# Sums of the second layers' weights and activations: from VectorE to GpSimd, gate halves to VectorE, activation sums begun at the last set's first output

## The chip, the core and the metric

One core of a Trainium2 chip runs the whole program. The metric is the device time of one execution in microseconds, of which three runs were timed. The engines are TensorE (PE in the rows, with its weight loads as PEld), VectorE (DVE), ScalarE (ACT), GpSimd (POOL) and SyncE (SP), which issues the transfers.

## What is computed

Attention with a memory term for 4 batches of 8 heads and 576 tokens, then two feed-forward blocks over all 2304 tokens. The change touches the end of the first block and the whole of the second:

```python
x = attn_out.transpose(0, 2, 1, 3).reshape(2304, 512)
h = x @ w_in                       # 512 -> 2048
x = maximum(0.01 * h, h) @ w_out   # 2048 -> 512
a, b = x @ w_a, x @ w_b            # 512 -> 1536 each
out = (a * b) @ w_out2             # 1536 -> 512
```

## The kernel before

Every fp32 matmul is made of three (`three`, L372 to L375): each operand is split into a rounded high half and a low half, and high x high, high x low and low x high are added in PSUM. A high half is a cast on ScalarE, a low half a subtraction (operand minus high half) on VectorE or GpSimd. So each tile that TensorE reads costs the other engines two steps, and those steps are what the order of the program is about.

The tokens go in two parts, 0 to 1023 and 1024 to 2303. The first block (`moe1`) runs over nine sets of a part with one or two of the eight groups of hidden features: `inward` gives hidden columns (leaky ReLU on ScalarE, L1077, then both halves), `outward` adds them into the result y of that part (L1095, VectorE). The last set is part 1 with groups 6 and 7: its outward part has eight outputs of 512 columns and four of 256. Beside it the program prepares the second block.

The second block (`moe2`) computes a and b for 1024 tokens of each part by a Strassen-like scheme with 7 products instead of 8. Matrices w_a and w_b come as 12 matrices of 2x2 blocks, b and a in turn; part by part the loop over q = 0 to 11 makes seven products (`product`), which take the right blocks or sums of blocks:

- `Matrices.make(m)` loads matrix m into the tile raw, forms the sums T1 to T4 of its blocks (L1257, four steps of 128x256), casts the high halves (L1260, ScalarE, tiles bhi or ahi) and subtracts the low halves (L1264, GpSimd, blo or alo), four pieces of 512 columns (p = 0 and 1 the blocks, 2 and 3 the sums), and writes the result to DRAM for the second pass over the tokens.
- `Sums` forms S1 to S4 out of the blocks of the activations (`total`, L1166) and the halves of the S and of A11, A12 and A22 (`hi` and `lo`, L1170 to L1178; L1175 for A, L1178 for S). `last` (L1145) makes the halves of a rest of 256 tokens of part 1.
- The product's results are added out of PSUM on VectorE (L1357, L1361 for product 1 on ScalarE). When an odd q is reached, `done` multiplies a and b (the gate, L1384) and `finish` casts the gate's high half (L1340) and subtracts the low half (L1342). `result` multiplies the gates with w_out2 and adds (L1419, VectorE); `Weights.final` makes the halves of w_out2 (L358 and L359).

What sets the order: every output or product is one tick. `after(k, fn)` puts a step into the program k ticks later, so each engine's queue is fixed by ticks; the engines then run through their queues in order and wait by semaphores. `jobs` is a list of steps of which `run(n)` issues n at each output or product.

PSUM has eight banks: four in turn for products and inward results (ring u), four for outputs (ring o). A bank is free again when VectorE or ScalarE has read it.

```python
for x_ in (("T1", "B12", "B11"), ("T2", "B22", "T1"), ("T3", "B22", "B12"), ("T4", "B21", "T2")):
    after(k, total(*x_))
for p in range(4):
    after(k + 1 + p, hi(p))
    after(k + 2 + p, low(p))
```

The slots of an even and an odd q in the first pass are "16572O3O4OO" and "1O6O5OO7234" (digits are products, O an output of the pair before).

Of the kernel before, what the change touches and what calls it, by code (L numbers as in the profile page):

```python
# [16 lines left out]
ALU = mybir.AluOpType  # L17
AX = mybir.AxisListType

B, H, S, D = 4, 8, 576, 64  # L20
# [92 lines left out]
def f32(ap):  # L113
    return ap.bitcast(F32)
# [3 lines left out]
def attention_moe_moe2(ctx: ExitStack, tc, kqT, qn, vn, m_prev, beta, w_in, w_out, w_a, w_b, w_o2, out):  # L118
    nc = tc.nc
# [10 lines left out]
    keep = const.tile([P, H], F32, name="keep")  # L130
# [16 lines left out]
    def after(k, fn):  # L147
        now[1] += 1
        heapq.heappush(tasks, (now[0] + k, now[1], fn))
# [969 lines left out]
    class Sums:  # L1119
# [22 lines left out]
        def last(self, y):  # L1142
            e = slice(1024, 1280)
            nc.scalar.copy(self.tail[:, 0], y[:, :, e])
            after(1, lambda: nc.gpsimd.tensor_tensor(self.tail[:, 1], y[:, :, e], f32(self.tail)[:, 0], ALU.subtract))  # L1145

        def jobs(self, y, places):

            at = self.at
            V, G = nc.vector, nc.gpsimd  # L1150

# [21 lines left out]
            def lo(x, eng):  # L1173
                if x[0] == "A":
                    fn = lambda: eng.tensor_tensor(at[x][:, 1], plain(x), f32(at[x])[:, 0], ALU.subtract)  # L1175
                else:
                    fn = lambda: [
                        eng.tensor_tensor(*two(at[x][:, 1, k], of(x, k), f32(at[x])[:, 0, k]), ALU.subtract) for k in range(2)  # L1178
                    ]
                return lambda: after(1, fn)  # L1180
# [16 lines left out]
    class Matrices:  # L1197
# [48 lines left out]
        def make(self, m):  # L1246
# [4 lines left out]
            lo = self.lo[x]  # L1251
            k = max(0, self.when + 5 - now[0])
            self.when = now[0] + k + 6

            def total(o, a, b):
                o, a, b = (self.pair(n) for n in (o, a, b))
                return lambda: nc.vector.tensor_tensor(o, a, b, ALU.subtract)  # L1257

# [11 lines left out]

            for x_ in (("T1", "B12", "B11"), ("T2", "B22", "T1"), ("T3", "B22", "B12"), ("T4", "B21", "T2")):
                after(k, total(*x_))
            for p in range(4):
                after(k + 1 + p, hi(p))
                after(k + 2 + p, low(p))
            if m < 11:
                after(k + 6, lambda: self.load(m + 1))
            after(k + 7, keep)

# [33 lines left out]
    def moe2(ps, sums, mats, spare):  # L1313
# [7 lines left out]
        for pr in range(2):  # L1321
# [16 lines left out]
            def finish(g, f, c, gf):  # L1338
                t = into(g, f)
                after(1, lambda: nc.scalar.copy(t[:, 0, c], gf))  # L1340
                eng = nc.vector if pr or (f, c.start) == (1, 0) else nc.gpsimd
                after(2, lambda: eng.tensor_tensor(t[:, 1, c], gf, f32(t)[:, 0, c], ALU.subtract))  # L1342

# [96 lines left out]
    with tc.manual_schedule():  # L1440
# [54 lines left out]
        for n, kind, g, w in moe1(ps, gates, lambda n: t31 if n == 1 else fourth(n), xs, y):  # L1495
# [3 lines left out]
            if n == len(SETS) - 1:  # L1499
                if (kind, g) == ("u", 6) and m == 1:  # L1500
# [4 lines left out]
                    mats.when = now[0]  # L1505
                if (kind, g) == ("u", 7) and m == 2:
                    m = 3
                    jobs.append(sums.jobs(ys[0], None)["1"])
                    mats.make(0)
                if kind == "o":  # L1510
                    m += 1
                if m == 9:
                    m = 10
                    while weights.items or weights.quarter or weights.spare:
# [6 lines left out]
                    sums.second()  # L1521
                    steps = sums.jobs(ys[0], {f"S{i + 1}": spares[i * 2 : i * 2 + 2] for i in range(4)})
                    jobs += [steps[k] for k in "ab65c2d7"]
                    mats.make(1)
            run(2)
            convert(w, 0.7 if n == 0 else 0.74)
# [4 lines left out]
        for pr, (kind, q, k) in moe2(ps, sums, mats, spares):  # L1531
            if (pr, kind, q, k) == (0, "P", 4, "1"):
# [6 lines left out]
                    "S4": [r[:, k * 512 : k * 512 + 512] for k in range(2, 4)],  # L1539
                })  # L1540
            if (pr, kind, q, k) == (0, "P", 6, "1"):
# [80 lines left out]
```

## Time and profile before

| | us |
|---|---|
| median of three runs | 1021.49 |
| lowest, highest | 1020.34, 1022.60 |
| the profiled execution | 1017.84 |
| its span, first to last instruction | 1016.1 |
| TensorE busy in the span | 991.3 |
| VectorE, ScalarE, GpSimd busy | 804.8, 424.2, 351.0 |

The profile is of one execution. An engine's busy time counts its instructions from start to end, a stretch in which an instruction of VectorE or GpSimd is held up by the other included. A wait is put down to the instruction that came last. The second block's products begin at about 590 us, its second pass over the tokens at about 780 us.

### The profile page before, as it was taken

What the parts mean: (1) busy time and instruction counts of PE and PEld (TensorE: products, weight loads), DVE (VectorE), ACT (ScalarE), POOL (GpSimd) and SP (SyncE); (2) the same over time, 40 slices, a digit from 0 to 9 for tenths busy, and PEclk for the clock granted to TensorE, in tenths of its full rate; (3) what the DMA queues carried; (4) which work ended last, traced back from release to release, by engine and by line L of the source; (5) the groups of instructions that cost most, each with busy time, mean ns of one, the idle gap of its engine ahead of it and who ended that gap; (6) DMA issues with size and microseconds to landing.
All of it is one profiled execution on the core that took longest, in us unless ns stands there. A gap on an engine that the chain in (4) does not pass through costs nothing. (4 is left out here: it accounts for less than half of the span.)

```text
span 1016.1 us, 14584 instructions
## 1 busy us (share of the span) xinstructions
PE 991.3 (98%) x5266; PEld 798.7 (79%) x5266; DVE 804.8 (79%) x1546; ACT 424.2 (42%) x947; POOL 351.0 (35%) x333
## 2 busy tenths in 40 slices
PE   9999999999999999999998989899998999999998
PEld 4666666788888888888887878778886888888887
DVE  6999998699798989898999585887787717647646
ACT  7988887565435242524235134323233121201201
POOL 6788777331102010202015156665555101001000
PEclk9999999999999999999999999999999999999999
DMA  7344432233435343434353344536555422432312
GB/s 228 106 133 138 154 107 73 63 125 114 145 107 174 112 137 115 160 120 145 106 162 117 118 188 175 215 123 224 221 186 188 159 111 93 149 132 94 138 50 104
DMA packets 41432, 139.88 MB, mean 138 GB/s; under 512 B 4752, under 2 KB 5520, under 8 KB 36752
## 3 DMA queue, kind: packets, MB, share of 16 engines
q1 hardware_dynamic: 41216, 138.95, 40.1%
q8 instruction: 41, 0.67, 0.3%
q14 instruction: 31, 0.25, 0.1%
q10 hardware_dynamic: 144, 0.00, 0.0%
HBM read 98.57 MB, written 40.37 MB: 137 GB/s over the span
## 5 line engine op out<-in xcount | busy, mean ns | idle before, releaser
L1357 DVE TENSOR_TENSOR gf<-b,gf 128x512 f32<-128x512 f32 x148 | 100.8, 687 | 63.5 <-PE b L375 58.8
L1419 DVE TENSOR_TENSOR xf<-b,xf 128x512 f32<-128x512 f32 (+1 forms) x91 | 61.7, 683 | 60.9 <-PE b L375 60.5
L1044 POOL TENSOR_TENSOR hl<-gf,hl 128x512 fp32r<-128x512 f32 (+1 forms) x20 | 28.3, 1415 | 233.3 <-ACT hl L1043 224.2
L373 PE MATMUL b<-xh,w 128*128 128x512 f32 x256 | 100.9, 394 | 0.0
L374 PE MATMUL b<-xh,w 128*128 128x512 f32 x256 | 99.7, 390 | 0.0
L375 PE MATMUL b<-xh,w 128*128 128x512 f32 x256 | 99.7, 389 | 0.0
L359 POOL TENSOR_TENSOR w<-bhi,w 128x512 fp32r<-128x512 f32 x24 | 35.8, 1492 | 181.2 <-ACT w L358 180.8
L373 PE MATMUL b<-xs,bhi 128*128 128x512 f32 (+1 forms) x216 | 79.7, 369 | 5.6 <-DVE gf L1357 5.1
L374 PE MATMUL b<-xs,bhi 128*128 128x512 f32 (+1 forms) x216 | 79.1, 366 | 0.0
L373 PE MATMUL b<-xs,ahi 128*128 128x512 f32 (+1 forms) x216 | 79.0, 366 | 0.0
L374 PE MATMUL b<-xs,ahi 128*128 128x512 f32 (+1 forms) x216 | 79.0, 366 | 0.0
L375 PE MATMUL b<-xs,blo 128*128 128x512 f32 (+1 forms) x216 | 79.0, 366 | 0.0
L375 PE MATMUL b<-xs,alo 128*128 128x512 f32 (+1 forms) x216 | 79.0, 366 | 0.0
L1077 ACT ACTIVATE gf<-b 128x512 f32<-128x512 f32 (+1 forms) x76 | 42.0, 553 | 82.5 <-PE b L375 80.8
L619 ACT ACTIVATE p<-p,stat 128x512 f32<-128x512 f32 (+3 forms) x128 | 71.0, 560 | 4.8 <-DVE stat L673 4.4
L373 PE MATMUL b<-hl,w 128*128 128x512 f32 (+1 forms) x176 | 65.8, 374 | 2.9 <-DVE xf L1095 2.9
L646 POOL TENSOR_SCALAR p<-p,stat,keep 128x128 f32<-128x128 f32 (+3 forms) x95 | 61.2, 656 | 16.1 <-DVE stat L634 13.7
L261 ACT ACTIVATE wh<-wraw 128x512 f32<-128x512 f32 x64 | 42.7, 668 | 55.2 <-DMA wraw<-in_w_o 21.5
L374 PE MATMUL b<-hl,w 128*128 128x512 f32 (+1 forms) x176 | 65.6, 373 | 0.0
L375 PE MATMUL b<-hl,w 128*128 128x512 f32 (+1 forms) x176 | 65.4, 372 | 0.0
L673 DVE CUSTOM_DVE_ANT_0 p<-b,mask 128x512 f32<-128x512 f32 (+3 forms) x128 | 57.6, 478 | 5.6 <-PE b L665 5.2
L302 DVE SCALAR_TENSOR_TENSOR wa<-wraw,wa 128x512 uint32<-128x512 uint32 x64 | 56.0, 875 | 1.4
(207 smaller groups left out, 2673.3 us busy)
## 6 DMA issues: line engine op xcount, KB each, us to landing
wraw<-in_w_in SPq DMA_DIRECT2D x16, 512.0 KB, 4.0
wraw<-in_w_out SPq DMA_DIRECT2D x16, 512.0 KB, 3.4
qraw<-in_qn SPq DMA_DIRECT2D x8, 768.0 KB, 7.0
wraw<-in_w_b SPq DMA_DIRECT2D x12, 512.0 KB, 3.4
wraw<-in_w_a SPq DMA_DIRECT2D x12, 512.0 KB, 3.7
plain<-wa SPq DMA_DIRECT2D x24, 256.0 KB, 3.7
wraw<-in_w_o SPq DMA_DIRECT2D x12, 512.0 KB, 3.7
raw<-plain SPq DMA_DIRECT2D x12, 512.0 KB, 3.3
```

The lines of the kernel that those rows point to most:

```text
L261: nc.scalar.activation(t["h"], self.raw[n][:, :, 1].bitcast(F32), AF.Abs)
L302: V.scalar_tensor_tensor(u["a"], raw[:, :, 1], 0xC0000000, u["a"], ALU.bitwise_and, ALU.bitwise_or)
L359: after(k + 6, lambda f=f: nc.gpsimd.tensor_tensor(w[:, 1, f], f32(stage), f32(w)[:, 0, f], ALU.subtract))
L373: nc.tensor.matmul(outp, l_hi, r_hi, start=start, stop=False)
L374: nc.tensor.matmul(outp, l_hi, r_lo, start=False, stop=False)
L375: nc.tensor.matmul(outp, l_lo, r_hi, start=False, stop=stop)
L619: nc.scalar.activation(t, t, AF.Exp, bias=s[:, 0, col : col + 1], scale=-1.0, accum_out=s[:, 1, col : col + 1])
L646: ENG[eng].tensor_scalar(live[p], live[p], stats[w % 3][:, 3, col : col + 1], k, ALU.mult, ALU.mult)
L673: nc.vector.tensor_tensor_reduce(one(p, [P, wd]), plan.tiles[banks[j]][:, c : c + wd], mask[:, off : off + wd], -0.125, BIG, ALU.add, ALU. ...
L1077: nc.scalar.activation(gf, hp[:, 0:n], AF.Prelu, alpha=0.01)
L1357: nc.vector.tensor_tensor(left[q, to], src, left[q, add], ALU.add)
L1419: nc.vector.tensor_tensor(y[:, i, c], op, y[:, i, c], ALU.add)
```

## The change

Six edits. The sums T1 to T4 go from VectorE to GpSimd and stand between the low halves of one matrix, over eight ticks. All gate low halves of the first pass go to VectorE (before, three of four were GpSimd's). For part 1 all S sums and their low halves go to GpSimd (`jobs` takes the engine as V). A's low halves and the tail's are two steps of 512 columns in place of one of 1024. Everything that prepares the second block begins at the last set's first output: the first matrix (before: at the inward part of group 7), the activation sums (before: at the sixth output), one job a tick in place of two; the second matrix follows at the seventh output. Minimum distances between matrices shrink by a tick.

```diff
@@ Sums.last
-            after(1, lambda: nc.gpsimd.tensor_tensor(self.tail[:, 1], y[:, :, e], f32(self.tail)[:, 0], ALU.subtract))
+            for k in (slice(0, 2), slice(2, 4)):
+                after(
+                    1 + 2 * k.start,
+                    lambda k=k: nc.gpsimd.tensor_tensor(self.tail[:, 1, k], y[:, k, e], f32(self.tail)[:, 0, k], ALU.subtract),
+                )
@@ Sums.jobs
-        def jobs(self, y, places):
+        def jobs(self, y, places, V):
...
-                    fn = lambda: eng.tensor_tensor(at[x][:, 1], plain(x), f32(at[x])[:, 0], ALU.subtract)
+                    fn = lambda: [
+                        eng.tensor_tensor(at[x][:, 1, k], plain(x)[:, k], f32(at[x])[:, 0, k], ALU.subtract) for k in range(2)
+                    ]
@@ Matrices.make
-            k = max(0, self.when + 5 - now[0])
-            self.when = now[0] + k + 6
+            k = max(0, self.when + 4 - now[0])
+            self.when = now[0] + k + 5
...
-                return lambda: nc.vector.tensor_tensor(o, a, b, ALU.subtract)
+                return lambda: nc.gpsimd.tensor_tensor(o, a, b, ALU.subtract)
...
-            for x_ in (("T1", "B12", "B11"), ("T2", "B22", "T1"), ("T3", "B22", "B12"), ("T4", "B21", "T2")):
-                after(k, total(*x_))
-            for p in range(4):
-                after(k + 1 + p, hi(p))
-                after(k + 2 + p, low(p))
+            steps = [
+                [hi(0), hi(1)], [low(0)], [total("T1", "B12", "B11"), total("T2", "B22", "T1")], [low(1), hi(2)],
+                [total("T3", "B22", "B12"), total("T4", "B21", "T2")], [hi(3), low(2)], [], [low(3)],
+            ]
+            for n, fns in enumerate(steps):
+                for fn in fns:
+                    after(k + n, fn)
             if m < 11:
-                after(k + 6, lambda: self.load(m + 1))
-            after(k + 7, keep)
+                after(k + 5, lambda: self.load(m + 1))
+            after(k + 8, keep)
@@ finish
-                eng = nc.vector if pr or (f, c.start) == (1, 0) else nc.gpsimd
-                after(2, lambda: eng.tensor_tensor(t[:, 1, c], gf, f32(t)[:, 0, c], ALU.subtract))
+                after(2, lambda: nc.vector.tensor_tensor(t[:, 1, c], gf, f32(t)[:, 0, c], ALU.subtract))
@@ the last set
-                if (kind, g) == ("u", 7) and m == 2:
-                    m = 3
-                    jobs.append(sums.jobs(ys[0], None)["1"])
-                    mats.make(0)
                 if kind == "o":
                     m += 1
                 if m == 9:
-                    m = 10
+                    mats.make(1)
+                if m == 3:
...
                     sums.second()
-                    steps = sums.jobs(ys[0], {f"S{i + 1}": spares[i * 2 : i * 2 + 2] for i in range(4)})
-                    jobs += [steps[k] for k in "ab65c2d7"]
-                    mats.make(1)
-            run(2)
+                    mats.make(0)
+                    steps = sums.jobs(ys[0], {f"S{i + 1}": spares[i * 2 : i * 2 + 2] for i in range(4)}, nc.vector)
+                    jobs += [steps[k] for k in "a1b65c2d7"]
+            run(2 if n == 0 else 1)
...
-                })
+                }, nc.gpsimd)
```

How the queues move, in three places (names: xf the result y, gf and raw sums and products, xs and hl halves that TensorE reads, b a PSUM bank). VectorE, the last set's outputs, before:

```order
L1095 TENSOR_TENSOR xf<-b_5869,xf 128x512
L1166 TENSOR_TENSOR gf<-xf 128x512 x2
L1166 TENSOR_TENSOR gf<-gf,xf 128x512 x2
L1257 TENSOR_TENSOR raw<-raw 128x256 x4
L1095 TENSOR_TENSOR xf<-b_5904,xf 128x512
L1178 TENSOR_TENSOR xs_5890<-gf,xs_5890 128x512 x4
L1095 TENSOR_TENSOR xf<-b_5928,xf 128x512
```

and now, from the first output on:

```order
L1095 TENSOR_TENSOR xf<-b_5780,xf 128x512
L1170 TENSOR_TENSOR gf<-xf 128x512 x2
L1095 TENSOR_TENSOR xf<-b_5809,xf 128x512
L1095 TENSOR_TENSOR xf<-b_5828,xf 128x512
L1170 TENSOR_TENSOR gf<-gf,xf 128x512 x2
L1095 TENSOR_TENSOR xf<-b_5846,xf 128x512
L1184 TENSOR_TENSOR xs_5801<-gf,xs_5801 128x512 x2
L1095 TENSOR_TENSOR xf<-b_5866,xf 128x512
```

Where twelve steps stood between the additions of three outputs, six now stand between those of five, and the sums of weights are gone from the queue.

GpSimd from the second matrix to the third, around the first products of the second block, before:

```order
L1264 TENSOR_TENSOR alo<-raw,ahi 128x512 x2
L1175 TENSOR_TENSOR xs_5890<-xf,xs_5890 128x1024
L1264 TENSOR_TENSOR alo<-raw,ahi 128x512 x2
L1175 TENSOR_TENSOR xs_5516<-xf,xs_5516 128x1024
L359 TENSOR_TENSOR w<-bhi,w 128x512
L1264 TENSOR_TENSOR blo<-raw,bhi 128x512 x4
```

and now:

```order
L1270 TENSOR_TENSOR alo<-raw,ahi 128x512
L1263 TENSOR_TENSOR raw<-raw 128x256 x2
L1270 TENSOR_TENSOR alo<-raw,ahi 128x512
L1263 TENSOR_TENSOR raw<-raw 128x256 x2
L1270 TENSOR_TENSOR alo<-raw,ahi 128x512
L1180 TENSOR_TENSOR xs_5516<-xf,xs_5516 128x512 x2
L1270 TENSOR_TENSOR alo<-raw,ahi 128x512
L359 TENSOR_TENSOR w<-bhi,w 128x512
L1270 TENSOR_TENSOR blo<-raw,bhi 128x512
L1263 TENSOR_TENSOR raw<-raw 128x256 x2
```

Two sums stand behind each matrix's first and second low half, and A22's low half (xs) before the last; the third matrix goes on in the same way, with a step of w before its last low half.

VectorE at the first gates (the end of q = 1), before:

```order
L1384 TENSOR_TENSOR gf<-raw,gf 128x512
L1357 TENSOR_TENSOR gf<-b_6135,gf 128x512
L1384 TENSOR_TENSOR gf<-gf 128x512
L1357 TENSOR_TENSOR gf<-b_6149,gf 128x512
L1384 TENSOR_TENSOR gf<-gf 128x512
L1357 TENSOR_TENSOR gf<-b_6163,gf 128x512
L1384 TENSOR_TENSOR gf<-gf 128x512
L1342 TENSOR_TENSOR hl_6132<-gf,hl_6132 128x512
```

and now:

```order
L1391 TENSOR_TENSOR gf<-raw,gf 128x512
L1364 TENSOR_TENSOR gf<-b_6138,gf 128x512
L1391 TENSOR_TENSOR gf<-gf 128x512
L1349 TENSOR_TENSOR hl_6133<-gf,hl_6133 128x512
L1364 TENSOR_TENSOR gf<-b_6151,gf 128x512
L1391 TENSOR_TENSOR gf<-gf 128x512
L1349 TENSOR_TENSOR hl_6147<-gf,hl_6147 128x512
L1364 TENSOR_TENSOR gf<-b_6164,gf 128x512
L1391 TENSOR_TENSOR gf<-gf 128x512
L1349 TENSOR_TENSOR hl_6133<-gf,hl_6133 128x512
L1349 TENSOR_TENSOR hl_6147<-gf,hl_6147 128x512
```

One low half behind four gates has become four, of which two stand before the fourth product's sum.

## Rows read from the trace of the kernel before

**Rows 1.** The page, span and part 1: busy us, share of the span, instructions.

```profile
span 1016.1 us, 14584 instructions
PE 991.3 (98%) x5266; PEld 798.7 (79%) x5266; DVE 804.8 (79%) x1546; ACT 424.2 (42%) x947; POOL 351.0 (35%) x333
```

**Rows 2.** Waits of TensorE from 540 us on: total us, times, longest.

```profile
PE b L373 <- DVE gf L1357: 5.1, 2, 3.1
PE b L374 <- DVE xs L1044: 3.7, 1, 3.7
PE b L373 <- DVE xf L1095: 2.9, 1, 2.9
PE b L373 <- DVE xf L1419: 1.4, 1, 1.4
PE b L375 <- POOL qs L1342: 1.4, 1, 1.4
PE b L373 <- ACT qs L1340: 1.1, 1, 1.1
PE b L373 <- DVE raw L1357: 0.4, 1, 0.4
PE b L375 <- DVE hl L1342: 0.2, 1, 0.2
```

**Rows 3.** Windows: length, TensorE busy us (instructions), granted clock, transfer share, GB/s.

```profile
555.00:560.00 5.00, 1.32 (x7) 0.98 0.00 0
560.00:565.00 5.00, 5.00 (x16) 0.68 0.97 326
```

**Rows 4.** Timeline, last set's inward part: start us, us, engine, line, step.

```profile
543.06 2.64 POOL L1175 TENSOR_TENSOR xs<-xf,xs 128x1024 fp32r<-128x1024 f32 x1 [1.09 <-ACT xs L1170]
543.36 2.63 DVE L1044 TENSOR_TENSOR hl<-gf,hl 128x256 fp32r<-128x256 f32 x1
547.06 3.61 DVE L1257 TENSOR_TENSOR raw<-raw 128x256 f32<-128x256 f32 x4
```

**Rows 5.** Timeline of TensorE: first matmuls of inward, outputs, q = 0, q = 1.

```profile
542.82 0.40 PE L373 MATMUL b<-xh,w 128*128 128x512 f32 x1
...
553.72 0.39 PE L373 MATMUL b<-hl,w 128*128 128x512 f32 x1
...
589.92 0.40 PE L373 MATMUL b<-xs,bhi 128*128 128x512 f32 x1
...
599.47 0.39 PE L373 MATMUL b<-xs,ahi 128*128 128x512 f32 x1
```

**Rows 6.** Timeline of VectorE, last set's outputs.

```profile
580.87 6.87 DVE L1178 TENSOR_TENSOR xs<-gf,xs 128x512 fp32r<-128x512 f32 x4
```

**Rows 7.** Timeline of VectorE, first pass of the second block.

```profile
645.58 6.27 DVE L1257 TENSOR_TENSOR raw<-raw 128x256 f32<-128x256 f32 x4
...
677.08 3.48 DVE L1166 TENSOR_TENSOR xf<-xf 128x512 f32<-128x512 f32 x2
```

**Rows 8.** Prices: timeline rows, a source line (ns min/median/max), two groups (busy us, mean ns).

```profile
757.93 0.68 DVE L1178 TENSOR_TENSOR xs<-raw,xs 128x512 fp32r<-128x512 f32 x1
675.37 1.78 DVE L1342 TENSOR_TENSOR hl<-gf,hl 128x512 fp32r<-128x512 f32 x1
592.33 1.30 POOL L1264 TENSOR_TENSOR alo<-raw,ahi 128x512 fp32r<-128x512 f32 x1 [5.14 <-ACT ahi L1260]
607.99 1.75 POOL L1342 TENSOR_TENSOR hl<-gf,hl 128x512 fp32r<-128x512 f32 x1 [1.92 <-ACT hl L1340]
L1257 DVE TENSOR_TENSOR raw<-raw x48: 409/422/2001, 547.1 to 744.6; 128x256 f32<-128x256 f32 x48
L1044 POOL TENSOR_TENSOR hl<-gf,hl 128x256 fp32r<-128x256 f32 x1 | 0.9, 854 | 3.8 <-DVE hl L1044 3.8
L1357 DVE TENSOR_TENSOR gf<-b,gf 128x512 f32<-128x512 f32 x148 | 100.8, 687 | 63.5 <-PE b L375 58.8
```

**Rows 9.** Timeline of VectorE, end of the first pass.

```profile
772.98 3.98 DVE L1166 TENSOR_TENSOR raw<-xf,raw 128x512 f32<-128x512 f32 x2
```

More of the change, by code (lines that the diff above doesn't have):

```diff
@@ L1144, in last @@
             nc.scalar.copy(self.tail[:, 0], y[:, :, e])
-            after(1, lambda: nc.gpsimd.tensor_tensor(self.tail[:, 1], y[:, :, e], f32(self.tail)[:, 0], ALU.subtract))
-        def jobs(self, y, places):
+            for k in (slice(0, 2), slice(2, 4)):
[4 more added lines that the diff above has]
+        def jobs(self, y, places, V):
             at = self.at
-            V, G = nc.vector, nc.gpsimd
+            G = nc.gpsimd
             def plain(x):
```

## Prediction

> **What bounds the kernel now.** I read the page first: TensorE is busy in 991.3 us of a span of 1016.1 [rows 1], so little but its idle stretches can be won. The waits of TensorE come second. From 540 us on they add up to 16.3 us in nine waits [rows 2]; the reader is to see that six of the eight rows name VectorE as what was waited for, one GpSimd and one ScalarE, and none a transfer. All of it lies in the part of the program that the change reorders. The windows come third: the granted clock reads 1.00 all through, except 0.98 and 0.68 in the ten microseconds after the first of these waits [rows 3]; 0.02 and 0.32 of 5 us each are 1.7 us lost at the lower of the two levels (1.2 GHz). It followed a wait of 3.7 us; the waits of 3.1 and 2.9 us were followed by none.
>
> The timelines come last, for why VectorE was late. A subtraction of two SBUF operands of 128x512 takes 0.68 us on VectorE when GpSimd is quiet and 1.78 us when it is not [rows 8]; four sums of weights (T1 to T4) took 3.61 us in one place and 6.27 us in another, although the median of one is 422 ns [rows 4, 7, 8]. VectorE's steps with one PSUM operand don't show this: 148 of them average 687 ns [rows 8]. So VectorE is late where its SBUF steps stand in bunches beside a busy GpSimd, and TensorE then lacks a half or a free bank.
>
> **The change, part by part.** TensorE's order is not touched. The sum is made against the profiled execution: 1017.84 us, with 1016.1 us of span. The three runs' median is 1021.49, 3.65 above it; I take the difference from the median.
>
> *The last set's inward part.* The high and low halves of A11 and the first matrix's sums go away from here: on VectorE 3.61 us of sums and a step held for 2.63 us behind a GpSimd step of 2.64 us [rows 4]. VectorE's low half that TensorE waited for began at about 559.1 us, its input long ready; with some 5 us less ahead of it and GpSimd nearly quiet, it is done before TensorE arrives. I take all of the wait, 3.7 us, and with it the 1.7 us of low clock: **-5.4**.
>
> *The last set's outputs.* They begin at 553.72 us [rows 5], and the activation sums now begin at the first of them instead of the sixth. Before, four low halves took 6.87 us beside GpSimd [rows 6], VectorE's additions stood behind them and TensorE ran out of banks. Four inward outputs take 553.72 - 542.82 = 10.90 us [rows 5], so one of 512 columns takes 2.72. Now each has one addition (0.69) and at most two SBUF steps, which with one GpSimd step in the way of each are 2 x 1.78: 4.2 us at worst for single outputs, 2.0 at best, and four banks to spread it over. I count no wait: **-2.9**. If the cover is gone, one bank's worth, 2.7, comes back.
>
> *The steady part, first pass.* Per pair of matrices VectorE loses eight sums (8 x 0.42) and gains three low halves (3 x 0.68), and the second pass's sums and halves leave it (16 steps). The bunches behind the waits named gf and raw of L1357 (the 6.27 us, and 3.48 us for two sums of activations [rows 7]) no longer stand on VectorE: 5.1 + 0.4 us, **-5.5**.
>
> *The end of the first pass.* Four waits, 1.4 + 1.4 + 1.1 + 0.2 = 4.1 us [rows 2]. One goes: the 3.98 us of S4's sum that held up the additions [rows 9] move to GpSimd. But after the last four products VectorE now makes all four low halves itself, in order: from the end of product 7 the steps are two sums, a gate, then three times sum, gate and half, so the half of product 2 is ready 9 x 0.68 = 6.1 us later, that of product 3 8.2 us later. TensorE wants them 4.5 and, once moving, 0.7 us after the former: waits of 1.6 and 1.4, plus up to 1.1 for one step of GpSimd's in the way. I take 3.6 for 4.1: **-0.5** (between -1.1 and +2).
>
> *What is late next: GpSimd at the start of the second layers.* With the waits gone TensorE starts these 3.7 + 1.7 + 2.9 = 8.3 us earlier, at 589.92 - 8.3 = 581.6 [rows 5], while GpSimd's work is later and longer. From the second matrix's first low half to the last of the third matrix its queue holds twelve steps of 512 columns and eight sums. A low half takes 1.30 us alone [rows 8]. No sum has run on GpSimd; the nearest row is a subtraction of 128x256 at 0.85 us [rows 8]. Below I bound it by VectorE's 0.42, above by 1.30 (twice the columns), and take 0.85, since the size is the same. So the queue is 12 x 1.30 + 8 x 0.85 = 22.4 us. The GPSIMD Engine Reference of the Trainium skill (4.1, Engine selection) says to keep two-input elementwise work on VectorE, GpSimd being about twice as slow; twice 0.42 is 0.84, an estimate by that page that leaves the sum as it is.
>
> It begins when S3's high half leaves ScalarE: output 8 ends at 553.72 + 8 x 2.72 = 575.5, then two additions, two sums and two high halves, about 580.3. A22's low half is the ninth and last of five long and four short steps, 9.9 us, and 0.45 for each of three VectorE steps that it alternates with (1.75 against 1.30 [rows 8]): ready at 591.5, wanted at 581.6 + 6 x 1.36 + 0.9 = 590.7 (a product is (599.47 - 589.92)/7 = 1.36 [rows 5]): 0.9. At the end of the second matrix's products VectorE's gates and halves meet this queue one by one: product 7 ends at 597.4, its sums at 598.8, then gate 599.9, sum 600.6, gate 602.5, half 604.3, sum 604.9, gate 606.0, half 606.7, sum 607.3; product 7 of the next matrix needs that sum's bank at 605.7: 1.6. ScalarE's copy of product 1, behind the gates' casts, adds 0.5. **+3.0** (with 0.42 for a sum 0.5, with 1.30 about 6).
>
> *The other four places where a pair of matrices ends.* There GpSimd's queue for the next matrix (4 x 1.30 + 4 x 0.85 + 1.30 = 9.9) is mostly done before the gates begin, 12.3 us after that matrix's call. Alone, VectorE's fourth sum is 6.9 us after product 7 and its bank wanted at 8.2: 1.3 to spare, and each step that meets a low half costs 1.1. One or two meet: 0.3 a place, **+1.2** (0 to 4 x 0.9, with two steps met at each). The tail's split halves, A's split halves and the wider spacing of the matrices' steps lie inside these queues; I cost them at nothing.
>
> Sum: -5.4 - 2.9 - 5.5 - 0.5 + 3.0 + 1.2 = -10.1. The span becomes 1006.0, the median 1021.49 - 10.1 = **1011.4 us**.
>
> **The rivals.** *GpSimd keeps up.* The sums run at VectorE's price or the queue starts earlier; the 14.3 us of the first four terms stay whole: 1007.2. For it: ScalarE's idle time there. Against: the one GpSimd subtraction of this size that ran alone took 0.85 us.
>
> *The early start doesn't happen.* The activation sums are issued at the first output, but stand on VectorE behind that output's addition and on ScalarE behind the matrix's casts. If GpSimd's sums hold those casts, the low halves bunch at the end again, and the 2.9 us stay: 1014.3. Against: the added steps have single outputs between them.
>
> *GpSimd sets the pace (slower than before).* The place is the end of each pair in the first pass. If a sum on GpSimd took 1.7 us, the start would cost 8 x 0.85 = 6.8 more, and a matrix's queue of 5.2 + 6.8 + 1.3 = 13.3 would overrun the gates' beginning at 12.3 by 1.0 at four places: 3.0 + 1.2 + 6.8 + 4.0 = 15.0 against 14.3. From there on it is slower; at 2.0, the most that one of these sums took on VectorE [rows 8], it is 3.0 + 1.2 + 9.2 + 4 x 2.2 - 14.3 = +7.9: 1029.4. Against it: 0.85 for the same size, and GpSimd's own steps stretch by 0.45 only beside VectorE's. SBUF — State Buffer of the Trainium skill (Who interferes with whom) says that of two such steps the later one blocks fully until the first is through; by that rule every gate or half of VectorE's that meets a sum on GpSimd waits it out. The trace agrees for VectorE, 1.78 for 0.68, which is 1.10 of a 1.30 step.
>
> **How the numbers follow.** Forecast 0.50, GpSimd keeps up 0.22, no early start 0.08, GpSimd's pace 0.20, of which 0.10 beyond the point of decision by more than 2 us, 0.07 around it, 0.03 short of it. A measurement here can tell about 0.2%, 2 us. Faster by more: 0.50 + 0.22 + 0.08 + 0.03 = 0.83; within 0.07; slower 0.10. The range: its low end is the second case with 1.1 off the pass's end, 1006; its high end takes the upper bounds of the start (+3.0) and of the four places (+2.4) and half that of the pass's end (+1.2), 1018. That leaves out the pace case alone.
>
> **What would show it.** In the changed profile TensorE's wait for xs of L1044 and the clock below 1.00 after it are gone; so is the wait for xf of L1095 in the last set; no wait for gf of L1357 follows a bunch on VectorE. A GpSimd sum of 256 columns reads 0.8 to 0.9 us alone. New waits stand near 590 us (A22's half, GpSimd) and near 605 us (a bank or a gate's half, VectorE), some 3 us in all, and about 3.6 us where the first pass ends. I am wrong if the waits after 540 us add up to more than 11 us, if the sums read above 1.3 us alone, or if a low clock stands at the first pass's end.

## The result, and the profile after

The changed kernel takes **1007.62 us** (median of four runs, 1006.16 to 1009.16); the kernel before, beside it, 1021.77 (four runs, 1020.34 to 1022.60). The ratio is 0.9863, 95% interval 0.9841 to 0.9885: 14.2 us, where 10.1 were forecast. The profiled execution takes 1009.16 us with a span of 1007.4.

The page of the changed kernel: the span, and of each engine the busy us, the share and the instructions.

```profile
span 1007.4 us, 14598 instructions
PE 990.8 (98%) x5266; PEld 799.0 (79%) x5266; DVE 771.1 (77%) x1500; ACT 425.1 (42%) x947; POOL 378.6 (38%) x386
```

TensorE is as busy as before [rows 1]; VectorE has given up 34 us and GpSimd taken on 28. What went is idle time. TensorE's waits from 540 us on (total us, times, longest):

```profile
PE b L375 <- DVE hl L1349: 2.0, 1, 2.0
PE b L373 <- ACT gf L1368: 1.7, 1, 1.7
PE b L375 <- DVE qs L1349: 1.1, 1, 1.1
PE b L373 <- ACT qs L1348: 0.8, 1, 0.8
```

These 5.6 us stand against 16.2 [rows 2] (the prediction's 16.3 adds the waits before rounding). The three largest waits of before (gf of L1357, xs of L1044, xf of L1095) have no successor. TensorE's first matmuls of the last set's outputs and of the second block's first product:

```profile
555.50 0.39 PE L373 MATMUL b<-hl,w 128*128 128x512 f32 x1
...
583.01 0.40 PE L373 MATMUL b<-xs,bhi 128*128 128x512 f32 x1
```

From the inward part (544.59) to those products it is 38.4 us, before 589.92 - 542.82 = 47.1 [rows 5]: 8.7 won in that stage, 8.3 forecast. The inward part itself began 1.8 us later than before, through longer waits in the first half of the program, which the change leaves alone; from the products to the end another 1.8 were won. 1.8 - 8.7 - 1.8 makes the 8.7 us between the two profiles. The medians differ by 14.2, since the profile of before stands at the low end of its runs (1017.84; in a later comparison 17 of them lay between 1016.1 and 1023.0) and that of after at the high end of its own. The runs of the kernel before scatter by 7 us, and their times go with the granted clock of the whole run. Over the 48 runs of the later comparisons the median is 1016.7 us at a clock of 1.000 (3 runs), 1018.8 at 0.998 (11), 1020.1 at 0.997 (6), 1020.5 at 0.995 (20) and 1022.0 at 0.993 (7). The profiled run is one of 0.998; the changed kernel's four stand at 0.997 and 0.998. So some 2 us of the 14.2 (an estimate, 1020.5 less 1018.8) go with low clock that a typical run of the kernel before has and its profile does not show; at which place of the program is not known.

The sums of weights on GpSimd (ns, least, median, most), and the windows (length, TensorE busy, clock, transfers) of the last set's inward part and of the end of the first pass:

```profile
L1263 POOL TENSOR_TENSOR raw<-raw x48: 720/740/1196, 558.9 to 735.2; 128x256 f32<-128x256 f32 x48
```

```profile
555.00:560.00 5.00, 5.00 (x23) 1.00 0.00 0
560.00:565.00 5.00, 5.00 (x23) 1.00 0.01 2
755.00:760.00 5.00, 1.80 (x6) 0.94 0.98 356
760.00:765.00 5.00, 4.27 (x10) 0.50 0.25 98
765.00:770.00 5.00, 5.00 (x21) 0.88 0.48 157
```

The low clock of [rows 3] is gone, and a longer one has come at the end of the first pass: 0.06, 0.50 and 0.12 of 5 us each are short by 3.4 us at 1.2 GHz. It comes with waits of 0.8, 1.1 and 2.0 us within six: in windows of a quarter of a microsecond the clock reads 0.74 from 759.25 us on, while TensorE stands in the third of them, and 0.50 after that. So 0.7 of the 3.4 lie inside that wait, and the work behind it lost 2.7. The third wait, on TensorE, VectorE and GpSimd:

```profile
760.73 0.80 PE L375 MATMUL b<-w,hl 128*128 128x512 f32 x1 [2.04 <-DVE hl L1349]
```

```profile
758.91 1.76 DVE L1349 TENSOR_TENSOR hl<-gf,hl 128x512 fp32r<-128x512 f32 x1
```

```profile
758.32 3.48 POOL L1184 TENSOR_TENSOR xs<-xf,xs 128x512 fp32r<-128x512 f32 x2 [5.05 <-ACT xs L1175]
```

A half of 0.68 us takes 1.76 beside a step that the change gave to GpSimd. The only other wait is ScalarE's doing, which holds a cast of w_out2 until its transfer has landed, with the copy of product 1 behind it in the queue:

```profile
698.72 0.62 ACT L358 CAST w<-bhi 128x512 fp32r<-128x512 f32 x1 [1.49 <-DMA bhi<-saved]
...
699.77 0.58 ACT L1368 COPY gf<-b 128x512 f32<-128x512 f32 x1
```

### The profile page after: what moved, and what is told of

It is laid out like the page before. It is cut to its first block, busy times and chain, and to the rows that moved or that the text cites. A ratio compares the mean times of both kernels' runs of the same rounds, so it can differ in the third digit from the quotient of the medians.

```text
span 1007.4 us, 14598 instructions
## 1 busy us (share of the span) xinstructions
PE 990.8 (98%) x5266; PEld 799.0 (79%) x5266; DVE 771.1 (77%) x1500; ACT 425.1 (42%) x947; POOL 378.6 (38%) x386
## 4 chain that ended last, share of the span: by engine, by line
PE 86%; DVE 5%; DMA 3%; POOL 2%; ACT 2%; issue 1%; SPq 0%; ACTq 0%; POOLq 0%; DVEq 0%
PE b L373 24%; PE b L375 24%; PE b L374 24%; PE b L724 4%; PE b L803 3%; PE b L665 3%; PE b L775 1%; DVE gf L1364 1%; DMA g<-xkept 1%; PE b L596 1%; DMA qraw<-in_qn 1%; PE b L693 1%; DMA bhi<-saved 1%; DVE gf L1391 1%; ACT p L619 1%
## 5 line engine op out<-in xcount | busy, mean ns | idle before, releaser
L1044 POOL TENSOR_TENSOR hl<-gf,hl 128x512 fp32r<-128x512 f32 (+1 forms) x20 | 28.3, 1415 | 234.9 <-ACT hl L1043 229.6
L375 PE MATMUL b<-w,hl 128*128 128x512 f32 (+1 forms) x145 | 57.0, 393 | 2.0 <-DVE hl L1349 2.0
```

The lines of the kernel that those rows point to most:

```text
L375: nc.tensor.matmul(outp, l_lo, r_hi, start=False, stop=stop)
```

## The experiments

The theory at the outset was the prediction's: each edit takes away its own waits, the early start those of the last set (8.3 us), sums and halves those of the first pass. Its rivals: one edit carries all; GpSimd's longer queue costs more than it gives. The first four undo one edit each.

**Sums back on VectorE**

```diff
-                return lambda: nc.gpsimd.tensor_tensor(o, a, b, ALU.subtract)
+                return lambda: nc.vector.tensor_tensor(o, a, b, ALU.subtract)
```

> The changed kernel with one thing undone: the sums T1 to T4 stand on VectorE again, in the places that they have now (two, then two). Theory (waits come where VectorE's steps of two SBUF operands stand in bunches beside a busy GpSimd): part of the first pass's waits for banks comes back, 1 to 5.5 us of them, so 1009 to 1013 us against 1007.6, with TensorE waiting for additions of L1364 near 645 us or at a pair's end, and sums that read up to 2 us. Rival (the early start alone carries the gain, the place of the sums is worth nothing): 1006 to 1008.5 us. Second rival (GpSimd's longer queue costs more than it gives): faster than the changed kernel by 1 us or more.

Measured: 1019.24 us, ratio to before 0.9992 (0.9978 to 1.0005). One word of the change undone, and the gain is gone, as far as can be measured. The waits behind additions, and the sums themselves:

```profile
PE b L373 <- DVE gf L1364: 7.8, 6, 2.0
PE b L373 <- DVE raw L1364: 2.4, 2, 2.0
```

```profile
L1263 DVE TENSOR_TENSOR raw<-raw x48: 407/1027/1517, 562.5 to 744.8; 128x256 f32<-128x256 f32 x48
```

In the spread chain, between GpSimd's halves, a sum on VectorE has a median of 1027 ns, more than the 740 that it takes on GpSimd in the same places; in the kernel before its median was 422 [rows 8]. The waits for banks stand where the theory put them, but it gave 5.5 us at most and 11.6 came.

**Gate halves back on GpSimd**

```diff
-                after(2, lambda: nc.vector.tensor_tensor(t[:, 1, c], gf, f32(t)[:, 0, c], ALU.subtract))
+                eng = nc.vector if pr or (f, c.start) == (1, 0) else nc.gpsimd
+                after(2, lambda: eng.tensor_tensor(t[:, 1, c], gf, f32(t)[:, 0, c], ALU.subtract))
```

> The changed kernel with one thing undone: three of four gate low halves of the first pass stand on GpSimd again, which now also has the sums of the weights. Theory: at the end of a pair of matrices a half on GpSimd stands behind up to four steps of 1.3 us and sums of 0.74 us, so outputs wait for it at one to five places: 1008 to 1014 us. Rival (VectorE's row of gates and halves is what makes the wait of 1.1 + 2.0 us and the low clock at the end of the first pass): that wait goes, with 2 to 6 us: 1002 to 1006 us. If neither place hangs on them: 1007 to 1008.5.

Measured: 1007.54 us, ratio 0.9874 (0.9858 to 0.9890), as the changed kernel. The end of the pass then waits 0.8 + 1.3 + 0.8 = 2.9 us for other halves, with the clock low again. In the changed kernel this edit is worth nothing that can be measured.

**Part 1's activation sums back on VectorE**

```diff
-                }, nc.gpsimd)
+                }, nc.vector)
```

> The changed kernel with one thing undone: the activation sums of part 1 and their low halves stand on VectorE again (at the end of the first pass, in the row of the last additions and halves). Theory: the additions of the last products and the halves of the last gates come later by the steps that stand ahead of them (each 0.7 to 1.8 us), so the wait at the end of the first pass, 3.9 us in the changed kernel, is 5 to 9 us, the clock stays low after it: 1009 to 1013 us. Rival (these steps fit into idle time of VectorE): 1007 to 1008.5 us.

Measured: 1008.94 us, ratio 0.9887 (0.9871 to 0.9902): 1.3 us above the changed kernel, with intervals that overlap, so the two can't be told apart. The waits at the end of the pass were 1.1, 1.1 and 1.0 us, fewer than the theory wanted; another 2.8 us stood in the pass.

**The old start** (the diff in part)

```diff
+                if (kind, g) == ("u", 7) and m == 2:
+                    m = 3
+                    jobs.append(sums.jobs(ys[0], None, nc.vector)["1"])
+                    mats.make(0)
...
-            run(2 if n == 0 else 1)
+            run(2)
```

> The changed kernel with one thing undone: the halves of A11, the first matrix and the activation sums begin where they did before (at the last inward part of group 7, and at the sixth output, two jobs a tick). The sums of weights stay on GpSimd. Theory (the two waits of the last set come from where these steps stand, bunched late): the wait for outputs' banks comes back, 2.9 us, and that of the inward part (3.7 us and 1.7 us of low clock) comes back in part, since GpSimd's steps stand there but VectorE's sums do not: 1010 to 1016 us. Rival (it was the sums on VectorE alone that made both waits): 1006.5 to 1008.5 us. If all of the gain hangs on the early start: 1020 us.

Measured: 1012.01 us, ratio 0.9919 (0.9904 to 0.9934): 4.4 us of the gain gone. Waits of 1.0 us in the inward part, 1.8 at 593 us and a clock of 0.83 from 590 to 600 make 4.5 of the 4.9 us between the two spans. The waits of the last set are much smaller than before the change all the same, so what the undone edits cost (11.6 + 4.4 + 1.3) is more than the change gained. They lean on each other; the next runs take them the other way, one edit alone upon the kernel before.

**The early start alone** (the change's lines in the last set, in the kernel before)

> The kernel before with one edit alone: everything that prepares the second block begins at the last set's first output, one job a tick. Sums of weights stay on VectorE, in their old chain. Theory as it stands after the first four runs (the early start, undone alone, cost 4.4 us; the sums, undone alone, 11.6): the waits of 3.7 and 2.9 us in the last set go with the low clock, and the waits of 5.1 us near 645 and 680 us stay: 5 to 8 us below the kernel before. Rival (the parts lean on each other: without the sums on GpSimd the early start only moves the bunch of sums, and a wait of 2 to 4 us stands at the first outputs or at the second block's first products): 0 to 3 us below.

Measured: 1039.39 us, ratio 1.0191 (1.0170 to 1.0212): 19 us slower, which no theory had. The waits of the last set did go; five others came:

```profile
PE b L375 <- POOL blo L1264: 21.2, 5, 4.7
```

One of them on GpSimd and TensorE; then the same place in the kernel before:

```profile
640.56 1.74 POOL L1264 TENSOR_TENSOR blo<-raw,bhi 128x512 fp32r<-128x512 f32 x1
642.26 1.72 POOL L1342 TENSOR_TENSOR hl<-gf,hl 128x512 fp32r<-128x512 f32 x1
643.94 2.94 POOL L1264 TENSOR_TENSOR blo<-raw,bhi 128x512 fp32r<-128x512 f32 x2
```

```profile
645.70 0.79 PE L375 MATMUL b<-xs,blo 128*128 128x512 f32 x1 [3.87 <-POOL blo L1264]
```

```profile
633.72 2.64 POOL L1264 TENSOR_TENSOR blo<-raw,bhi 128x512 fp32r<-128x512 f32 x2 [0.19 <-ACT bhi L1260]
638.07 1.75 POOL L1342 TENSOR_TENSOR qs<-gf,qs 128x512 fp32r<-128x512 f32 x1 [1.71 <-ACT qs L1340]
```

In the kernel before, b's low halves are through before the gates' halves come; here they stand among them. The reason is in the distances. `make` begins a matrix at least 11 ticks after the one ahead, and a pair has 22 ticks for two matrices, so a lag that arises at the start is never made up. Counted in ticks, from the fourth matrix on a matrix begins 4 to 6 ticks after the call in the kernel before, 8 to 10 here, 0 to 2 in the changed kernel, whose distance is 9 (two constants shrink by a tick each, so the distance by two). The early start makes the first two matrices close neighbours, and the lag of that place stays for the whole pass. The prediction's sum has no term for the distances.

**Sums on GpSimd alone, with the spread chain and the distances of 9**

```diff
@@ Matrices.make, all of it as in the changed kernel; nothing else
+            k = max(0, self.when + 4 - now[0])
+            self.when = now[0] + k + 5
...
+                return lambda: nc.gpsimd.tensor_tensor(o, a, b, ALU.subtract)
```

> The kernel before with one edit alone: the sums T1 to T4 on GpSimd in the spread chain. Start, gate halves and activation sums as before (three of four gate halves on GpSimd). Theory: it carries most of the gain, since undone alone it cost 11.6 of 14.2 us; the bunches on VectorE near 547, 645 and 680 us are gone, and what is left is the last set's wait for banks (2.9 us) and the pass's end: 6 to 11 us below the kernel before. Rival (what undoing it cost was VectorE overloaded by sums and halves together, so that the sums alone are worth only the 5.5 us of the steady part): 4 to 6 us below. Rival 2 (GpSimd with sums and halves sets the pace): 0 to 3 us below, or above.

Measured: 1006.43 us, ratio 0.9864 (0.9844 to 0.9884): the whole gain with one function changed, where the theory gave 6 to 11 us. The other edits (the start, the gates' halves, the activation sums, the split halves) add nothing to it that can be measured. Its longest waits, and its windows where the kernel before had the low clock and at the end of the pass:

```profile
PE b L375 <- POOL qs L1344: 1.3, 1, 1.3
PE b L373 <- DVE gf L1359: 1.2, 2, 0.8
PE b L373 <- ACT qs L1342: 1.1, 1, 1.1
PE b L374 <- POOL qs L1044: 0.6, 1, 0.6
```

```profile
560.00:570.00 10.00, 10.00 (x46) 1.00 0.51 210
750.00:760.00 10.00, 7.34 (x27) 0.92 0.65 232
```

The wait for xf of L1095 is gone though the activation sums begin at the sixth output as before; of the 3.7 us for xs of L1044 0.6 is left, without a low clock, though the first matrix begins where it did.

**Both undone: sums on VectorE, gate halves on GpSimd**, the rest as changed

> The changed kernel with two things undone: sums T1 to T4 on VectorE, three of four gate halves on GpSimd. Beside the run with the sums alone on VectorE (1019.2 us) it tells whether that run was slow because VectorE had both. Theory (load of VectorE: 8 x 0.42 us of sums and 3 x 0.68 of halves per pair of matrices): most of the banks' waits of 1 to 2 us near 645, 680, 711 and 743 us go: 1010 to 1014 us. Rival (the sums' places alone make the waits, the halves are worth nothing, as in the changed kernel): 1017 to 1020 us.

Measured: 1014.75 us, ratio 0.9940 (0.9922 to 0.9958). That is just above the theory's range and clear of the rival's. The load of VectorE counts: with the halves off it the sums cost 7.2 us, with the halves on it 11.6.

**Three outputs behind the last products of the pass**

```diff
-                text = ("16572O3O4OO", "1O6O5OO7234")[a] if g else "1657234"
+                text = ("16572O3O4OO", "1O657234OOO" if q == 11 else "1O6O5OO7234")[a] if g else "1657234"
```

> The changed kernel with another order of TensorE at the end of the first pass: three outputs of the pair before follow the last four products of the last matrix in place of standing ahead of them. They read halves that are long ready, so TensorE has 3 x 1.36 = 4.1 us of work while VectorE makes the last gates and halves. Theory (the waits of 0.8, 1.1 and 2.0 us there, and the half clock after them, which is 3.4 us, are one cause: products that end too close to the outputs that read them): both go, 4 to 7 us below the changed kernel: 1000.5 to 1004 us. Rival 1 (the additions of those outputs stand in VectorE's row too and push the gates back as much as TensorE gains): the waits shrink by 1 to 2 us and the clock still falls: 1005 to 1008 us. Rival 2 (the low clock comes at that place whatever waits there): 3 to 4 us below: 1003.5 to 1004.5.

Measured: 1007.60 us, ratio 0.9875 (0.9856 to 0.9894). No gain: waits of 0.8 and 2.9 us stood in the old place and the clock fell as before. By its timeline GpSimd's steps stretched VectorE's row; a later run shows a second reason.

**The engine of the sums alone**, in the old chain, at the old distances

```diff
-                return lambda: nc.vector.tensor_tensor(o, a, b, ALU.subtract)
+                return lambda: nc.gpsimd.tensor_tensor(o, a, b, ALU.subtract)
```

> The kernel before with the sums T1 to T4 issued on GpSimd, in the old chain (four sums, then the halves one a tick) and with the old distances of 11 ticks from matrix to matrix. Of the run that moved the sums with the spread chain and 9 ticks (1006.4 us) it keeps the engine alone. Theory (the engine is what counts: no bunch of VectorE's steps is lengthened by a busy GpSimd): 1006 to 1010 us. Rival (with four sums of 0.74 us ahead of the first high half and a start four products later, the low halves of the next matrix come too late, as in the run with the early start alone, where five waits of 4.2 us for the halves of b stood): waits for blo or alo of 1 to 4 us at most pairs, 1012 to 1035 us.

Measured: 1010.20 us, ratio 0.9898 (0.9881 to 0.9916): 10 us, the larger part. Its longest waits, and its windows:

```profile
PE b L374 <- DVE xs L1044: 3.3, 1, 3.3
PE b L375 <- POOL qs L1342: 1.3, 1, 1.3
PE b L373 <- DVE gf L1357: 1.2, 2, 0.9
```

```profile
560.00:570.00 10.00, 8.86 (x32) 0.83 0.79 288
```

The waits for xf of L1095 and most of those for gf of L1357 go with the engine alone. The last set's inward part keeps its wait, 3.3 us, and 1.7 of low clock: four sums in a row on GpSimd hold other steps up there as those on VectorE did. A step of VectorE's that takes 0.68 us in the kernel before takes 2.77, and ScalarE waits 2.4 and 3.2 us for GpSimd's own halves behind the sums. Spread, they cost 0.6 us, as the run of the whole function shows; the first two matrices begin at the same ticks in both kernels, so there it is the chain and not the distance.

**The distance alone**

```diff
-            k = max(0, self.when + 5 - now[0])
-            self.when = now[0] + k + 6
+            k = max(0, self.when + 4 - now[0])
+            self.when = now[0] + k + 5
```

> The kernel before with the distance from matrix to matrix at 9 ticks in place of 11 and nothing else. Counted in ticks, before starts every matrix from the fourth on four ticks after it could, with 9 it starts at once: its sums and halves stand 5.4 us earlier against the products. Theory (waits come from VectorE's sums beside GpSimd's steps, wherever in the pair they stand): the waits of 5.1 us near 650 and 680 us move or halve, the last set's stay: 1016 to 1021 us. Rival (the late start is what set the bunch of sums on top of the gates, and 9 ticks alone dissolve it): 1010 to 1014 us.

Measured: 1040.92 us, ratio 1.0203 (1.0183 to 1.0224): 21 us slower, and neither theory had that. Starting earlier harms as much as starting later. VectorE, and TensorE's wait:

```profile
649.76 6.89 DVE L1257 TENSOR_TENSOR raw<-raw 128x256 f32<-128x256 f32 x4
656.58 1.75 DVE L1342 TENSOR_TENSOR qs<-gf,qs 128x512 fp32r<-128x512 f32 x1
```

```profile
658.38 0.80 PE L375 MATMUL b<-w,qs 128*128 128x512 f32 x1 [3.46 <-DVE qs L1342]
```

Four sums now stand ahead of a gate's half, which outputs wait for; in the kernel before, the half is made first and the sums come at 645.58 [rows 7]:

```profile
642.00 1.78 DVE L1342 TENSOR_TENSOR qs<-gf,qs 128x512 fp32r<-128x512 f32 x1
```

Three delays were tried with the sums on VectorE: 0 to 2 ticks here, 4 to 6 in the kernel before, 8 to 10 with the early start alone. Of these only the middle one kept the pass free of waits for halves up to its end.

**Three outputs last, and the activation sums of part 1 from the last product on**

```diff
-                jobs += [steps[x] for x in {"1": "1b", "6": "6", "5": "5", "4": "7c234"}.get(k, "")]
+                jobs += [steps[x] for x in {"4": "1b657c234"}.get(k, "")]
```

> The changed kernel with three outputs after the last products of the first pass, as in the run before it, and with all activation sums of part 1 issued from the last product on in place of from the first. In that earlier run VectorE's row of gates and halves took 5 us longer than its steps alone, since GpSimd made those sums beside it. Theory (GpSimd's sums beside that row are what makes the last waits): the row is some 3 to 5 us shorter, the wait of 2.9 us and the half clock after it go: 1000 to 1003 us. Rival 1 (VectorE's row is late by itself): the wait stays at 2 to 3 us with the low clock: 1006 to 1008 us. Rival 2 (the sums come too late for part 1's first products): a wait of TensorE for halves of S near 765 to 775 us, 2 us or more: 1003 to 1008 us.

Measured: 1006.96 us, ratio 0.9870 (0.9851 to 0.9889). VectorE's steps keep their own pace now up to the last half, which takes 1.75 us beside GpSimd again, and the wait stays, 2.0 us. ScalarE shows why the row is late before that:

```profile
754.38 0.62 ACT L1348 CAST qs<-gf 128x512 fp32r<-128x512 f32 x1 [5.41 <-PE b L375]
```

The gates' halves live in three tiles that take turns, two for each pair of matrices. Outputs moved behind the products still read one of them, and the cast that fills it must wait until TensorE has done so; VectorE stood 3.45 us behind that cast.

**A quiet end**: TensorE's order as changed, part 1's sums from the first output on, product 3's half ahead of product 4's addition

```diff
+                a, b = {(1, 512): (1, 4), (1, 0): (0, 1)}.get((f, c.start), (1, 2)) if (pr, g) == (0, 5) else (1, 2)
...
-            if (pr, kind, q) == (0, "P", 11):
+            if (pr, kind, q, k) == (0, "O", 5, 0):
+                jobs += [steps[x] for x in "1b657c234"]
```

> The changed kernel with two edits at the end of the first pass, TensorE's order as in the changed kernel. The activation sums of part 1 begin at the first output after the last products, so that GpSimd is quiet beside VectorE's row of additions, gates and halves; and in that row the half of product 3, which the first output needs, stands ahead of product 4's addition and gate, that of product 7, needed four outputs later, behind them. (The run with three outputs moved behind the products showed the row at its own pace, 0.69 us a step, up to the third gate, and then a cast that waited until TensorE had read the tile that it writes; here no output stands behind the products.) Theory (the waits of 0.8, 1.1 and 2.0 us come from steps of that row held by GpSimd's and from two steps that need not stand ahead): half 3 is done 4 us earlier, waits there add up to less than 1.5 us and the half clock after them, 3.4 us, goes: 1000 to 1003 us. Rival 1 (the waits shrink, the clock falls all the same): 1004 to 1006 us. Rival 2 (the sums of part 1 come too late for its first products): new waits near 765 to 775 us, 1006 us or more.

Measured: 1007.55 us, ratio 0.9869 (0.9847 to 0.9891). At the end of the pass it does what the theory says: 0.7 us of waits in place of 3.9, at full clock. Its longest waits, its windows, and ScalarE's queue thereafter:

```profile
PE b L373 <- ACT gf L1369: 5.0, 2, 3.3
PE b L375 <- DVE qs L1350: 0.5, 1, 0.5
PE b L373 <- ACT qs L1349: 0.2, 1, 0.2
```

```profile
750.00:760.00 10.00, 9.32 (x40) 1.00 0.66 239
760.00:770.00 10.00, 10.00 (x57) 1.00 0.65 238
770.00:780.00 10.00, 6.73 (x29) 0.95 0.01 2
780.00:790.00 10.00, 10.00 (x39) 0.88 0.55 193
```

```profile
773.86 0.62 ACT L1175 CAST xs<-raw 128x512 fp32r<-128x512 f32 x1 [5.12 <-POOL raw L1170]
...
777.63 0.60 ACT L1369 COPY gf<-b 128x512 f32<-128x512 f32 x1
```

The gain was given back 20 us later: part 1's last sum came late from GpSimd, the cast that waits for it held ScalarE's queue, and product 1's copy behind it came 3.3 us after TensorE wanted its bank; 1.7 us of low clock followed. Part 1's sums were started at the last matrix's first product, at its last and at the first output, and none of the three came out ahead; a start at the last product without moving the outputs was not tried. No kernel beat the changed one beyond its interval.

## Why the prediction was right, and where its reasons were not

The time lies in the range and the sign is right. VectorE's sums beside a busy GpSimd made the waits, in bunches of four and, with the chain spread, in pairs too (1019.2 us); taking them off VectorE took the waits away, and that edit alone is worth 10 us. How much of it is the stretching of steps and how much VectorE's plain load no run separates. Of the prediction's three signs of being wrong one came, the low clock at the first pass's end; the waits add up to 5.6 us and not to more than 11, and a sum took 0.74 us and not more than 1.3. Point by point:

- **The last set's inward part, -5.4.** The wait and the low clock went. The term put that down to A11's halves and the sums leaving the place, which is enough: with the early start alone the wait is gone. It isn't needed: the spread chain on GpSimd, at the old place, leaves 0.6 us and no low clock.
- **The last set's outputs, -2.9.** Gone. The early start that the term names takes this wait away by itself too (in the run of 1039.4 us), but it isn't needed: with the sums on GpSimd and the old start the wait is gone as well, twice shown (1010.2 and 1006.4 us).
- **The steady part, -5.5.** Gone; with the engine alone 1.2 us of waits for gf stayed. This term had the cause right.
- **The end of the first pass, -0.5.** The waits were 3.9 us against 3.6 foreseen, and the walk through VectorE's row named the right halves. What failed is that no low clock was counted, 2.7 us of lost work: the range for that place went up to +2, for waits alone. The waits alone don't decide it: waits of 1.1, 1.4 and 0.2 us were followed by no low clock at this place in the kernel before, but the same waits (1.1, 1.3 and 0.2) by 1.7 us of it in the runs of 1006.4, 1010.2 and 1040.9 us.
- **What is late next, +3.0.** Nearly nothing. A sum took 0.74 us, not 0.85, so the eight of two matrices took 0.9 less. The second matrix's chain began at 580.60 (580.3 forecast), but the products, in a program 1.8 us late by then, at 583.01 and not 581.6, so the queue had 1.1 us more. TensorE idled 0.4 us there, in short gaps that the list of waits leaves out. The waits foreseen for A22's half and for a bank near 605 us didn't come.
- **The other pairs' ends, +1.2.** One wait of 1.7 us, by ScalarE behind a transfer and not by VectorE's halves: the size about right by luck, the mechanism not.
- **The distances, no term.** They decide where a matrix's steps fall against the gates all through the pass. With the sums on VectorE the new distances alone cost 21 us, and the early start at the old ones costs 19. What they are worth once the sums are on GpSimd is open: neither the spread chain at the old distances nor the changed kernel at them was run.

Set against the terms, the profile of after gives -5.4, -2.9, -5.5, -0.2 of waits and +2.7 of clock at the pass's end, +0.4 and +1.7: -9.2. The two profiles from 540 us on show 10.5 us won (8.7 + 1.8), the forecast's sum was 10.1. So it came near by errors that cancel, 2.6 too much at the start, 3.0 too little at the end of the pass and 0.5 at the other ends, and 1.3 us stay untraced. The rest of the way to the medians' 14.2 is where each profile lies among its own runs (3.9 and 1.5 us), less the 1.8 of the first half. That is what the forecast of 1011.4 missed, more than its terms: it took what one profile shows off the median of runs that, by the clocks above, had more low clock than the profiled one.

Of the rivals, GpSimd keeps up (1007.2) came nearest: next to nothing was late at the start, though a sum did not run at VectorE's price. That its number meets the median is luck, since the 14.3 us that it counts lie behind 540 us, where the two profiles show 10.5. GpSimd sets the pace needed 1.7 us for a sum; 740 ns speaks against it, and from 540 us on TensorE waits for GpSimd nowhere in the changed kernel. Whether a queue half as long again would still fit was not tried. The GPSIMD Engine Reference of the Trainium skill (4.1, Engine selection) advises VectorE for two-input elementwise work, with GpSimd about twice as slow. Per step that is near (740 ns to 422, 1.75 times); for this kernel the measurement decides the other way, by 10 us, since VectorE was the engine that TensorE waited for. SBUF — State Buffer of the Trainium skill (Who interferes with whom) says that a VectorE step with two SBUF inputs contends with a GpSimd step that reads SBUF, for ports that are an exclusive lock; the trace agrees, with 1.76 us for a half of 0.68.

## What to carry to other kernels

Two engines that lengthen each other's steps are to be weighed as a pair: a step can be cheaper on the slower engine (740 ns against 1027 in the same places). Undo each edit alone, and also make each alone; here one function held the whole gain and two other edits, alone, cost 2% each. One of them, the early start, did so because a minimum distance in a schedule with no slack keeps every lag that it is given. When a wait is removed, name the tile, the bank and the queue that its place passes on to: twice the repaired end of the pass was held somewhere else.

## What the runs showed that was not expected

- The clock fell to 1.2 GHz in the last of three short waits (0.8, 1.1 and 2.0 us within six), as it had after one of 3.7, and stayed there longer: 2.7 us of work lost against 1.7. After 1.1, 1.4 and 0.2 us at the same place in the kernel before [rows 2] it had not fallen, while after the same waits there it did in three other runs. What tells these apart was not measured.
- Moving the bunch of four sums by 4 to 6 ticks, either way, costs 19 to 21 us: TensorE's waits from 540 us on are about 26 us in either run, and the low clock takes 17 us, of which 2 to 3 lie inside waits, against 16 and 2 in the kernel before. Most of the waits of 2.4 to 4.7 us there are followed by a low clock, while those of 3.1 and 2.9 us in the kernel before [rows 2] were not.
- Sums on VectorE in pairs, spread between GpSimd's halves, took 1027 ns at the median, in the bunches of four of the kernel before 422, although the longest, 2001 ns, stood in one of these [rows 8]. Spread out, more of them met the other engine.
